# GpSimd instead of VectorE for the copies of weight slots in a linear-attention and mixture-of-experts kernel

## The chip, the cores and the metric

One core of a Trainium2 chip. The metric is the time of one execution on the device in microseconds (us); lower is better. Each result lists the granted TensorE clock (1.0 is full).

## The reference, cut to what matters

```python
kv  = einsum('bhsd,bhse->bhde', k, v)            # 8 sentences, 8 heads, 576 rows, 64 wide
out = einsum('bhsd,bhde->bhse', q, kv)
x   = out / sqrt(mean(out*out) + 1e-6) * g_norm  # -> 8 x 576 x 512
e   = argmax(mean_over_rows(x) @ w_gate)         # one expert per sentence, of 8
h   = maximum(x @ w1[e], 0)                      # w1[e]: 512 x 1024
y   = gate_weight * (h @ w2[e])                  # w2[e]: 1024 x 512
```

With the inputs used, the experts of sentences 0 to 7 are 4 4 7 6 5 1 3 1. Sentence 1 repeats sentence 0's expert and sentence 7 repeats sentence 5's.

## The kernel before

The weights of a sentence live in one of three slots of W1 and W2. Expert numbers are only known on the chip. So before each load of weights, the kernel copies the slot of one of the two preceding sentences into the sentence's own slot, and then loads from HBM over it, unless the expert is the same as one of the two:

```python
def s_w(b, i):                                   # b: sentence, i: W1 or W2
    own = b % NW
    W = (W1, W2)[i]
    cond = None
    if b > 0:
        if b > 1 and i == 0:
            st[b]["sv"] = nc.values_load(st[b]["src"][0:1, 0:1],
                                         engines=(mybir.EngineType.DVE,), ...)
        sv = st[b].get("sv", 0)                  # sentence 1: always slot 0
        for h in range(2):
            n = W.shape[2] // 2
            nc.vector.tensor_copy(W[:, own, h * n:(h + 1) * n],
                W[:, ds(sv, 1), h * n:(h + 1) * n].rearrange("p o c f -> p (o c) f"))
        for e in evs[max(0, b - 2):b]: ...       # cond: expert differs from both
    ...
        nc.gpsimd.dma_start(W[:, own, :, fs], (moe_w1, moe_w2)[i][ds(ev, 1), :, fs]..., cond=cond)
```

The kernel gives each engine its instructions in the order of a fixed list (`ORDER`). Steps, with the names that the profile gives their outputs: `qr` (VectorE re-packs q, SBUF to SBUF), `o` (attention output out of PSUM), `xT` (VectorE: `o` times `rs`, two SBUF inputs), `tw` and `ts` (VectorE: the gate's product and sum; `tw` has two SBUF inputs), `lg` (GpSimd's power operation, from which VectorE makes the gate), `m_1` and `m_2` (TensorE: the two matrix products with W1 and W2, profile lines L352 and L392).

```python
nc.vector.scalar_tensor_tensor(out=part(s["xT"][:, c, :], h), in0=s["o", c, h], scalar=gcol,
                               in1=part(s["rs", c], h), op0=ALU.mult, op1=ALU.mult, ...)   # xT
nc.vector.tensor_tensor(tw, wg, s["pl"][:, 0:NP].unsqueeze(2).to_broadcast(...), ALU.mult)  # tw
nc.gpsimd.tensor_tensor(lg, base, st[b]["dl"], ALU.pow)                                    # lg
```

Of the kernel before, what the change touches and what calls it, by code (L numbers as in the profile page):

```python
# [50 lines left out]
def kernel(  # L51
# [11 lines left out]
    nc = tc.nc  # L63
# [28 lines left out]
    st = [dict() for _ in range(B)]  # L92
# [209 lines left out]
    def s_w(b, i):  # L302
# [3 lines that stand above are left out]
        if b > 0:  # L306
            if b > 1 and i == 0:
                st[b]["sv"] = nc.values_load(
                    st[b]["src"][0:1, 0:1], engines=(mybir.EngineType.DVE,), min_val=0,
                    max_val=NW - 1,  # L310
                    skip_runtime_bounds_check_because="it is one of two numbers of slots")
            sv = st[b].get("sv", 0)
            for h in range(2):
                n = W.shape[2] // 2
                nc.vector.tensor_copy(  # L315
                    W[:, own, h * n:(h + 1) * n],
                    W[:, ds(sv, 1), h * n:(h + 1) * n].rearrange("p o c f -> p (o c) f"))
            for e in evs[max(0, b - 2):b]:
                c = evs[b] != e
                cond = c if cond is None else s_logical_and(cond, c)  # L320
        ev = evs[b]
        nh = {0: 4, B - 1: 2}.get(b, 1) if i == 0 else 1
        n = W.shape[3] // nh
        for h in range(nh):
            fs = slice(h * n, (h + 1) * n)
            nc.gpsimd.dma_start(W[:, own, :, fs], (moe_w1, moe_w2)[i][ds(ev, 1), :, fs]  # L326
                                .rearrange("o (c p) f -> p (o c) f", p=P), cond=cond)
# [93 lines left out]
    def emit(tok):  # L421
# [10 lines left out]
        elif f == "R":  # L432
            cast_first(c)
        elif f == "P":
            st[0]["row"] = sm.tile([1, E], F32, tag="row", name="row")
            nc.vector.tensor_copy(st[0]["row"], st[0]["pg"])
            ps0.__exit__(None, None, None)
            psp[0] = ctx.enter_context(tc.tile_pool(name="ps", bufs=2,
                                                    space=bass.MemoryType.PSUM))
            first[0] = False  # L440
        elif f == "K":
            s_kv(b, [c] if b == 0 else range(NP))
        elif f == "C":
            s_tc(b, c)
        elif f == "G":
            if (b, c) == (0, 1):
                s_row()
            else:
                (s_gate, s_gate2, s_gate3, s_gate4)[c](b)
        elif f == "Q":  # L450
            s_qr(b)
        elif f == "W":
            s_w(b, c)
        elif f == "L":
            load_qkv(b, 1, only=(c,))
        elif f == "T":
            s_qt(b, c, x)
        elif f == "O":
            s_o(b, c, h, x)
        else:  # L460
            dict(M=s_m, X=s_x)[f](b, c, h)
# [33 lines left out]
```

## Time and profile before

| | before |
|---|---|
| time, three runs | 194.69, 194.96, 196.69 us |
| span of the profiled run, clock | 191.0 us, 0.995 |
| busy: TensorE, VectorE, ScalarE, GpSimd | 170.8, 110.8, 106.6, 50.4 us |

The prediction below shows the lines and reads them.

### The profile page before, as it was taken

To read this page: it belongs to the slowest core of one execution; us is meant where nothing else is said; L and a number is where in the kernel's file an instruction comes from. 1 tells how busy PE (TensorE), PEld (TensorE's weight loads), DVE (VectorE), ACT (ScalarE), POOL (GpSimd) and SP (SyncE) were. 2 spreads that over 40 slices of the span, in tenths; PEclk is the share of its full clock that TensorE was granted. 3 is DMA by queue.
4 is the path that set the end of the run, shared out by engine and by line. 5 is a ranking of instruction groups with operands and counts; after the bars stand their busy time and mean duration, and the time that the engine had idled before them with its cause. 6 is when DMAs were issued, how large, how long until landed. Compare 5 with 4: busy or idle time off the path is not lost.

```text
span 191.0 us, 4338 instructions
## 1 busy us (share of the span) xinstructions
PE 170.8 (89%) x1691; PEld 113.0 (59%) x1691; DVE 110.8 (58%) x289; ACT 106.6 (56%) x168; POOL 50.4 (26%) x64
## 2 busy tenths in 40 slices
PE   0297787998999999899999999999999999999991
PEld 0253255775578755686568746867586568457541
DVE  2437374878878795585565785697754482332010
ACT  2146107767877767676666655675257656316512
POOL 7670098018305130016127020311022103000000
PEclk9999999999999999999999999999999999999998
DMA  5999999999999999999999999999999799062045
GB/s 157 194 202 205 201 200 189 206 208 201 229 239 246 205 207 240 255 228 203 221 259 235 205 217 243 264 188 170 239 260 187 154 158 210 18 160 76 0 113 134
DMA packets 37030, 36.91 MB, mean 193 GB/s; under 512 B 2706, under 2 KB 30354, under 8 KB 37010
## 3 DMA queue, kind: packets, MB, share of 16 engines
q0 software_dynamic: 29328, 26.30, 86.4%
q1 hardware_dynamic: 7394, 9.98, 18.2%
q10 hardware_dynamic: 288, 0.36, 0.7%
q8 instruction: 13, 0.21, 0.4%
q14 instruction: 7, 0.06, 0.1%
HBM read 61.88 MB, written 9.44 MB: 373 GB/s over the span
## 4 chain that ended last, share of the span: by engine, by line
PE 58%; DMA 23%; DVE 6%; issue 5%; ACT 4%; POOL 2%; POOLq 0%; DVEq 0%
PE ps_m L352 27%; PE ps_m L392 21%; DMA W<-in_moe_w_dram 12%; DMA qt<-in_q_dram 7%; DMA kt<-in_k_dram 4%; DVE o L179 3%; ACT sq L212 3%; PE ps_a L224 3%; PE ps_a L207 2%; PE ps_m L379 2%; PE ps_a L160 2%; DVE W L315 1%; PE ps_a L192 1%; POOL qt L103 1%; DVE qr L174 1%
## 5 line engine op out<-in xcount | busy, mean ns | idle before, releaser
L352 PE MATMUL ps_m<-xT,W 128*128 128x288 f16 x512 | 68.2, 286 | 1.2 <-DMA W<-in_moe_w_dram 1.2
L392 PE MATMUL ps_m<-W,hT 128*128 128x512 f16 x256 | 60.7, 379 | 0.0
L352 PEld LDWEIGHTS <-W 128*128 128x128 f16 x512 | 49.4, 98 | 13.9 <-DMA W<-in_moe_w_dram 1.6
L359 ACT ACTIVATE hT<-ps_m 128x576 f16<-128x576 f32 x51 | 33.2, 652 | 21.5 <-PE ps_m L352 21.3
L392 PEld LDWEIGHTS <-hT 128*128 128x128 f16 x256 | 24.2, 98 | 24.5 <-ACT hT L359 0.6
L326 POOL DMA_DIRECT2D W<-in_moe_w_dram x20 | 12.5, 628 | 74.6 <-DMA W<-in_moe_w_dram 16.5
L363 ACT ACTIVATE ot<-ps_m,gates 128x512 f32<-128x512 f32 (+1 forms) x26 | 17.0, 656 | 18.2 <-PE ps_m L392 12.9
L228 ACT ACTIVATE rs<-ps_a,epsc 128x576 f32<-128x576 f32 x28 | 20.5, 741 | 7.2 <-PE ps_a L224 6.7
L237 DVE SCALAR_TENSOR_TENSOR xT<-o,gcol,rs 128x576 f16<-128x576 f32 x28 | 22.4, 811 | 3.5 <-ACT rs L228 3.4
L212 ACT ACTIVATE sq<-ps_a 128x576 f16<-128x576 f32 x28 | 17.9, 648 | 10.6 <-PE ps_a L207 10.5
L179 DVE COPY o<-ps_a 128x576 f32<-128x576 f32 x20 | 15.0, 757 | 15.2 <-ACT sq L212 14.9
L277 POOL TENSOR_TENSOR lg<-base,dl 128x8 f32<-128x8 f32 x8 | 14.7, 1836 | 27.2 <-DVE src L296 17.7
L365 DVE TENSOR_SCALAR ot<-ps_m,gates 128x512 f32<-128x512 f32 (+1 forms) x14 | 9.4, 673 | 18.5 <-PE ps_m L392 16.6
L315 DVE COPY W<-W 128x2048 f16 (+1 forms) x28 | 19.3, 695 | 1.4 <-DVE src L296 0.5
L179 ACT COPY qT<-ps_a 128x576 f16<-128x576 f16 x15 | 9.5, 636 | 10.7 <-PE ps_a L160 10.7
L356 DVE TENSOR_SCALAR hT<-ps_m 128x576 f16<-128x576 f32 x13 | 9.8, 755 | 8.7 <-PE ps_m L352 8.7
L192 PEld LDWEIGHTS <-kt 96*64 96x64 f16 x384 | 7.5, 116 | 9.9 <-ACT kt L179 5.8
L224 PE MATMUL ps_a<-sq,ones 128*128 128x288 f16 x56 | 11.1, 286 | 2.1 <-DVE o L179 2.0
L207 PE MATMUL ps_a<-qT,kvb 128*128 128x288 f16 x56 | 11.3, 286 | 1.2 <-DVE o L179 0.8
L103 POOL DMA_DIRECT2D kt<-in_k_dram x10 | 7.5, 750 | 12.7 <-PE ps_m L352 12.4
L224 PEld LDWEIGHTS <-ones 128*128 128x128 f16 x64 | 6.0, 99 | 7.9 <-issue 3.2
L160 PEld LDWEIGHTS <-qr 96*128 96x128 f16 x144 | 8.7, 98 | 2.7 <-issue 0.4
(75 smaller groups left out, 138.1 us busy)
## 6 DMA issues: line engine op xcount, KB each, us to landing
W<-in_moe_w_dram POOLq DMA_DIRECT2D x14, 1024.0 KB, 14.1
out_dram<-ot SPq DMA_DIRECT2D x24, 192.0 KB, 5.7
qt<-in_q_dram POOLq DMA_DIRECT2D x7, 576.0 KB, 14.6
kt<-in_k_dram POOLq DMA_DIRECT2D x7, 576.0 KB, 10.4
vt<-in_v_dram POOLq DMA_DIRECT2D x7, 576.0 KB, 16.1
out_dram<-ot SPq DMA_DIRECT2D x39, 64.0 KB, 5.6
out_dram<-ot SPq DMA_DIRECT2D x16, 128.0 KB, 5.2
W<-in_moe_w_dram POOLq DMA_DIRECT2D x4, 256.0 KB
```

Of the source, the lines that this page charges most:

```text
L179: nc.scalar.copy(out, in_) if x else nc.vector.tensor_copy(out, in_)
L207: nc.tensor.matmul(po[:, i, 0:HS], kvb[:, b % 2, c, :], s["qT"][:, c, i * HS:(i + 1) * HS], start=True, stop=True)
L212: nc.scalar.activation(part(s["sq", c], h), po, AF.Square)
L224: nc.tensor.matmul(pm[:, i if h is None else 0, 0:HS], ones, s["sq", c][:, i * HS:(i + 1) * HS], start=True, stop=True)
L228: nc.scalar.activation(part(s["rs", c], h), pm[:, 0:2 if h is None else 1, 0:HS], AF.Abs_reciprocal_sqrt, bias=epsc)
L237: nc.vector.scalar_tensor_tensor(out=part(s["xT"][:, c, :], h), in0=s["o", c, h], scalar=gcol, in1=part(s["rs", c], h), op0=ALU.mult, op1= ...
L277: nc.gpsimd.tensor_tensor(lg, base, st[b]["dl"], ALU.pow)
L315: nc.vector.tensor_copy(W[:, own, h * n:(h + 1) * n], W[:, ds(sv, 1), h * n:(h + 1) * n].rearrange("p o c f -> p (o c) f"))
L352: nc.tensor.matmul(ph[:, i, 0:HS], w1[:, c, fb * P:(fb + 1) * P], s["xT"][:, c, i * HS:(i + 1) * HS], start=(c == 0), stop=(c == 3))
L359: nc.scalar.activation(two(s["hT"][:, fb, :]), ph[:, :, 0:HS], AF.Relu)
L363: nc.scalar.activation(out, in_, AF.Copy, scale=gates[:, b:b + 1])
L392: nc.tensor.matmul(po[:, 0, :], s["hT"][:, fc, t * P:(t + 1) * P], w2[:, fc, :], start=(fc == 0), stop=(fc == 7))
```

## The change

Its intent: take 19 us of copies off VectorE and give them to an engine that is idle three quarters of the time, and that issues the loads behind the copies anyway. The whole diff:

```diff
                 st[b]["sv"] = nc.values_load(
-                    st[b]["src"][0:1, 0:1], engines=(mybir.EngineType.DVE,), min_val=0,
+                    st[b]["src"][0:1, 0:1], engines=(mybir.EngineType.Pool,), min_val=0,
 ...
             for h in range(2):
                 n = W.shape[2] // 2
-                nc.vector.tensor_copy(
+                nc.gpsimd.tensor_copy(
                     W[:, own, h * n:(h + 1) * n],
                     W[:, ds(sv, 1), h * n:(h + 1) * n].rearrange("p o c f -> p (o c) f"))
```

## The prediction

In it and in the expectations further down, "the port" and "the lock" stand for one thing: an instruction of VectorE and one of GpSimd that overlap hold each other up. The trace of the kernel before showed this in the power operation alone (1.67 and 2.48 us), and the ten waits of 1 us are my estimate.

> **What bounds the kernel now.** I read the busy row of each engine first. VectorE, which the change relieves, is busy 58% of the 191.0 us span, GpSimd 26%, TensorE 89%. So the first question is whether VectorE's copies matter to anyone. The slices show which two things are full.
>
> ```profile
> PE   0297787998999999899999999999999999999991
> DVE  2437374878878795585565785697754482332010
> POOL 7670098018305130016127020311022103000000
> DMA  5999999999999999999999999999999799062045
> ```
>
> One slice is 4.8 us. From about 33 us TensorE is at nine or more nearly always, and the DMA engines are at nine up to about 145 us. VectorE is never full for long. The kernel is bound by TensorE, with the loads close behind it; from 140 us on there is only TensorE. The view of waits says how often TensorE stood still for a load of weights:
>
> ```profile
> PE ps_m L352 <- DMA W<-in_moe_w_dram: 1.2, 2, 0.9
> PE ps_a L224 <- DVE o L179: 2.0, 3, 1.1
> ```
>
> Two waits for weights, 1.2 us in all. By windows they are one of 0.9 us at 78 us (sentence 2's first weights) and one of 0.3 us at 137 us (sentence 5's). The waits on VectorE's o copy lie mostly (1.5 of 2.0 us) before 50 us, near or before the first weight copy at 48.8 us, so most of them cannot be the copies' fault.
>
> Next, the copies, the loads and the power operation on GpSimd, in the list of groups:
>
> ```profile
> L315 DVE COPY W<-W 128x2048 f16 (+1 forms) x28 | 19.3, 695 | 1.4 <-DVE src L296 0.5
> L326 POOL DMA_DIRECT2D W<-in_moe_w_dram x20 | 12.5, 628 | 74.6 <-DMA W<-in_moe_w_dram 16.5
> L277 POOL TENSOR_TENSOR lg<-base,dl 128x8 f32<-128x8 f32 x8 | 14.7, 1836 | 27.2 <-DVE src L296 17.7
> ```
>
> There are 28 copies (seven sentences, two matrices, two halves), 0.695 us each, 19.3 us of VectorE. GpSimd sits idle 74.6 us before its weight loads. Setting VectorE's and GpSimd's timelines side by side, every load of weights from sentence 2 on is issued 0.3 to 0.6 us after the second half of its copy ends. So the copy gates each load, and the copy itself starts when VectorE's program order comes to it. The chain of waits shows the one place where that matters for the end:
>
> ```profile
> 124.19 0.32 DVE o L179
> ...
> 124.86 0.70 DVE W L315
> 125.56 0.02 issue
> 125.58 0.70 DVE W L315
> ...
> 126.92 10.18 DMA W<-in_moe_w_dram
> 137.11 0.05 issue
> 137.16 2.87 PE ps_m L352 x22
> ```
>
> The columns are start, length, what. Two copies, 0.6 us to the issue, a 10.18 us load, and TensorE begins sentence 5 the moment it lands. After it TensorE is busy without a gap of note to the end, so what is lost here is lost from the time.
>
> [...] No GpSimd copy is in this trace, but there are three small stand-ins.
>
> ```profile
> 3.52 0.23 POOL masks.py:197 MEMSET ident<- 128x128 f16 x1
> 3.81 0.29 POOL masks.py:199 TENSOR_SCALAR_AFFINE_SELECT ident<-ident 128x128 f16<-128x128 f16 x1
> 0.46 0.11 POOL L479 MEMSET const-uint8-127<- 128x1 uint8 x1
> ```
>
> From one element (0.093 to 0.113 us, mean 0.104) to 128 elements (0.225 and 0.295 us in the list of groups) the slope is 0.95 ns and 1.50 ns an element[...]. [...] the power operation takes 1.67 us when undisturbed, and 2.48 us where VectorE's four qr copies (59.03 to 60.18 us) lie on it.
>
> ```profile
> 59.23 2.48 POOL L277 TENSOR_TENSOR lg<-base,dl 128x8 f32<-128x8 f32 x1 [1.42 <-DVE src L296]
> 122.54 1.67 POOL L277 TENSOR_TENSOR lg<-base,dl 128x8 f32<-128x8 f32 x1 [7.49 <-DVE src L296]
> ```
>
> **The change part by part.** Removed from VectorE: 28 x 0.695 = 19.3 us, leaving 110.8 - 19.3 = 91.5 us, 48% of the old span. Added to GpSimd: 28 copies of 2048 elements. At 0.95 ns: 0.104 + 2048 x 0.00095 = 2.05 us; at 1.50 ns: 3.18 us. I choose 2.05, since the copy has nothing to compute, and keep 3.18 as the bad case. 28 x 2.05 = 57 us, so GpSimd goes from 50.4 to about 108 us, 55% of the span. It is not full, but it also issues all loads of q, k, v and weights in order, so a copy pair of 4.1 us stands ahead of whatever comes next on it.
>
> Moved: the copy no longer waits for VectorE's program order, but for GpSimd's, and starts as soon as GpSimd gets to it. For each load I took GpSimd's last act before it in the old timeline, added about 0.4 us to read the slot number (0.29 us is what such a register load takes in the trace), 4.1 us for the pair and 0.6 us to the issue:
>
> - Sentence 2, first weights: power ends near 61, issue near 66.2; it was 65.45. Late by 0.8. The loads ahead of it (issued 51.77, landing after up to 20.4 us) keep the queue fed to about 71, so nothing is lost.
> - Sentence 3: the k load's issue ends 83.8, so 88.9; it was 86.78. Late by 2.1. The queue is fed to 91.3 (82.97 + 8.3). With some 2.7 us between an issue and its first data (my estimate, below), slack is 1.8, so 0.3 us is lost.
> - Sentence 4: late by some 3.5, with two older loads queued ahead and TensorE not there before 117 us. Nothing.
> - Sentence 5: source number at 122.38, power to 124.21, then 124.6 + 4.1 + 0.6 = 129.3; it was 126.92. Late by 2.4, of which up to 0.4 may hide, so 2.0.
> - Sentences 6 and 7: late by 1 to 3, but TensorE comes to them more than 3 us after they land, and is itself pushed back by the 2 us. Nothing.
>
> That sentence 5 has no slack is shown by the DMA in windows of 1 us (last two columns: DMA share, GB/s). The last v load is issued at 114.28 and lands after 15.4 us, at 129.7, and the rate sags there already:
>
> ```profile
> 127.00:128.00 1.00, 1.00 (x6) 0.49 (x5) 0.86 (x4) 0.97 (x2) 0.73 (x1) 1.00 1.25 194
> 128.00:129.00 1.00, 1.00 (x7) 0.43 (x5) 0.97 (x3) 0.27 (x1) 0.00 (x0) 1.00 1.22 135
> 129.00:130.00 1.00, 1.00 (x8) 0.65 (x7) 0.52 (x1) 0.58 (x2) 0.00 (x0) 1.00 0.86 147
> 130.00:131.00 1.00, 1.00 (x11) 0.54 (x8) 0.39 (x1) 1.00 (x2) 0.87 (x1) 1.00 1.16 201
> ```
>
> So the queue ran nearly dry about 2 us after the issue at 126.92 and filled again near 130: that is where the 2.7 us comes from.
>
> Then the port. About ten of the 28 xT operations of VectorE (two SBUF inputs each, 0.811 us) should meet a GpSimd copy and wait 1 us on average: 10 us back of the 19 us saved. They stand ahead of the o copies that free TensorE's banks, so I put 0.5 us on the path. Sum: 2.0 + 0.3 + 0.5 = 2.8 us, 194.96 + 2.8 = 197.8 us.
>
> **The rivals.** First, a gain: the copies leave VectorE's queue, o copies and gates come sooner. For it: the chain has a copy pair of 1.20 us at 56.5 us in front of an o copy. Against: the saved time there runs into the wait at 78 us, which is set by the backlog of loads, and TensorE waited on o only 0.5 us after 50 us. If a GpSimd copy took only 1 us[...], sentence 5 would issue at 127.2, and the time stays at 195 or falls by half a us. Second, a copy of 3.18 us: sentence 5 then issues at 131.5, late by 4.6; sentence 3 at 91.2, 2.6 lost; with more port waits, 7 to 8 us, about 202 us; GpSimd busy about 140 us and nearly the second bound. Third, the load is hidden anyway: if the queue still has work at 130 us, nothing changes at all, and the time stays within 0.5 us of 195.
>
> **Range and chances.** I give 2.05 us a copy (1.8 to 2.3) about half, 3 us a quarter, 1.2 us or less an eighth. That makes a middle of 197.8, and 195.2 to 202.0 as the range. Slower by over 2% begins at 198.9, which needs copies of about 2.5 us or more, or port waits of 2 us on the path: 0.34. Faster by over 2% would need a bound that VectorE sets, and none is seen: 0.03.
>
> **What will show it.** The copy's duration in the groups on GpSimd: 2.05 right, 1 or 3 wrong. The issue of sentence 5's first weights near 129.3 instead of 126.9, and TensorE's wait on weights there about 2.3 instead of 0.3 us. The mean of xT above 0.811 us, or VectorE's idle time in front of it grown. If TensorE's new idle time names o or xT rather than weights, the port is the larger cost; if the new wait is at sentence 2 or 3, my backlog estimate is wrong; if TensorE waits for nothing new, the third rival holds.

## The result and the profile after

The changed kernel took 204.46 us in the median of four runs (202.63 to 206.85), against 194.82 us (four runs). The ratio is 1.048, 95% interval 1.036 to 1.061: slower. A ratio here is the mean time of one kernel's fast runs over that of the other's fast runs of the same rounds, so it is not quite the ratio of the medians.

The slices of the span, changed kernel (one slice is 5.1 us):

```profile
PE   0298796998795999999969999999989999899992
DVE  1346354777997546675591789473953254021010
POOL 7750276009973599009965974089539901870000
PEclk9999767999997999999999999999999999999999
```

GpSimd is now often full. New and not foreseen is the last row: the clock granted to TensorE sags in slices 4 to 6 (about 20 to 35 us), before any copy of weights runs, and once more in slice 12. Then the groups of instructions:

```profile
L315 POOL COPY W<-W 128x2048 f16 (+1 forms) x28 | 56.3, 2016 | 7.4 <-PE ps_m L352 5.4
L237 DVE SCALAR_TENSOR_TENSOR xT<-o,gcol,rs 128x576 f16<-128x576 f32 x28 | 33.5, 1216 | 5.4 <-ACT rs L228 5.4
```

In the kernel before, the line of xT reads:

```profile
L237 DVE SCALAR_TENSOR_TENSOR xT<-o,gcol,rs 128x576 f16<-128x576 f32 x28 | 22.4, 811 | 3.5 <-ACT rs L228 3.4
```

A copy takes 2.02 us on average (its median by line is 1.90), as predicted. But xT, whose code did not change, went from 811 to 1216 ns. The chain of waits, changed kernel, shows where that matters:

```profile
50.00 3.58 DVE qr L174 x4
53.58 3.84 DVE xT L237 x6
...
59.62 3.09 DVE tw L244
62.74 0.21 DVE ts L246
62.98 0.47 DVE qT L179
63.49 0.58 PE ps_a L207 x2
```

From 50 to 63 us the path to the end runs through VectorE. In the kernel before it runs through TensorE there up to 55 us, and through VectorE only from 55.8 to 58.9. The operation tw on 32 elements a partition takes 3.09 us; its median is 0.19. The timeline of the changed kernel shows what lay beside it:

```profile
58.92 3.73 POOL L315 COPY W<-W 128x2048 f16<-128x2048 f16 x2
59.62 3.08 DVE L244 TENSOR_TENSOR tw<-wg,pl 128x32 f32<-128x32 f32 x1
```

tw begins during sentence 1's second pair of GpSimd copies and ends, at 62.70, with it. TensorE's waits in the changed kernel (us in total, times, longest) name VectorE more than the weights:

```profile
PE ps_a L207 <- DVE qT L179: 3.4, 2, 2.3
PE ps_m L352 <- DMA W<-in_moe_w_dram: 0.5, 2, 0.3
```

**Stages.** To see where time went I cut each trace at the first m_1 matmul of each sentence in TensorE's timeline. Uneventful stages repeat to a few hundredths of a us, whatever the total does and on whichever of three chips the rounds ran, so this is a far finer instrument than the total. "Again" means a second trace of the same kernel; the last column of each row ends the span.

| us | start to 0 | 0 to 2 | 2 to 3 | 3 to 4 | 4 to 5 | 5 to 6 | 6 to 7 | 7 to end | span |
|---|---|---|---|---|---|---|---|---|---|
| before | 30.85 | 47.62 | 19.31 | 19.48 | 19.90 | 17.83 | 16.08 | 19.98 | 191.0 |
| before, again | 36.44 | 47.84 | 19.30 | 19.48 | 19.98 | 17.82 | 16.05 | 19.97 | 196.9 |
| changed | 33.59 | 53.27 | 21.35 | 19.48 | 21.32 | 17.98 | 16.68 | 19.95 | 203.6 |
| changed, again | 31.02 | 50.36 | 21.03 | 19.67 | 21.34 | 17.82 | 17.53 | 19.98 | 198.7 |

Three readings. The start varies by 5.6 us between two traces of the *unchanged* kernel, with half clock and later first loads in the slow one; that is chance. Of the changed kernel's loss, 2.5 to 2.7 us lie between sentences 0 and 2 where the clock stays full (5.4 to 5.7 where it sags), 1.7 to 2.0 between 2 and 3, 1.4 between 4 and 5, and 0.6 to 1.5 between 6 and 7. At full clock that is 7.7 us of span (198.7 against 191.0).

The stretch from 0 to 2 hides part of the loss. From sentence 0 to 1 alone, at full clock throughout, the kernel before takes 25.14 us and the changed kernel (again) 28.90: 3.8 us more. In the next stage 1.0 us comes back (22.48 against 21.46), because there the kernel before waits 0.9 us for sentence 2's weights.

### The profile page after: what moved, and what is told of

The parts are those of the page before. It is cut to its first block, busy times and chain, and to the rows that moved or that the text cites. A ratio compares the mean times of both kernels' runs of the same rounds, so it can differ in the third digit from the quotient of the medians.

```text
span 203.6 us, 4362 instructions
## 1 busy us (share of the span) xinstructions
PE 178.0 (87%) x1691; PEld 115.6 (57%) x1691; DVE 108.5 (53%) x261; ACT 107.0 (53%) x168; POOL 106.3 (52%) x92
## 4 chain that ended last, share of the span: by engine, by line
PE 59%; DMA 14%; DVE 12%; issue 5%; POOL 5%; ACT 3%; POOLq 1%; ACTq 0%
PE ps_m L352 24%; PE ps_m L392 17%; DMA W<-in_moe_w_dram 10%; POOL W L315 4%; DMA vt<-in_v_dram 3%; DVE o L179 3%; PE ps_a L207 2%; PE ps_a L224 2%; DVE xT L237 2%; ACT sq L212 2%; PE ps_a L149 2%; PE ps_m L379 2%; PE ps_kv L149 2%; PE ps_a L192 2%; DVE qr L174 2%
## 5 line engine op out<-in xcount | busy, mean ns | idle before, releaser
L352 PE MATMUL ps_m<-xT,W 128*128 128x288 f16 x512 | 70.7, 292 | 0.5 <-DMA W<-in_moe_w_dram 0.5
L315 POOL COPY W<-W 128x2048 f16 (+1 forms) x28 | 56.3, 2016 | 7.4 <-PE ps_m L352 5.4
L352 PEld LDWEIGHTS <-W 128*128 128x128 f16 x512 | 50.5, 100 | 14.6 <-issue 0.8
L237 DVE SCALAR_TENSOR_TENSOR xT<-o,gcol,rs 128x576 f16<-128x576 f32 x28 | 33.5, 1216 | 5.4 <-ACT rs L228 5.4
L207 PEld LDWEIGHTS <-kvb 128*128 128x128 f16 x64 | 5.9, 103 | 9.8 <-issue 6.5
L160 PE MATMUL ps_a<-ident,qr 96*128 96x96 f16 x144 | 10.4, 209 | 1.1 <-ACT o L179 1.1
```

What stands on the lines that cost most here:

```text
L207: nc.tensor.matmul(po[:, i, 0:HS], kvb[:, b % 2, c, :], s["qT"][:, c, i * HS:(i + 1) * HS], start=True, stop=True)
L315: nc.gpsimd.tensor_copy(W[:, own, h * n:(h + 1) * n], W[:, ds(sv, 1), h * n:(h + 1) * n].rearrange("p o c f -> p (o c) f"))
L352: nc.tensor.matmul(ph[:, i, 0:HS], w1[:, c, fb * P:(fb + 1) * P], s["xT"][:, c, i * HS:(i + 1) * HS], start=(c == 0), stop=(c == 3))
```

## The experiments

I had two theories. **Late loads**: the long copy on GpSimd delays the loads queued behind it. **The port**: while a GpSimd copy runs, VectorE's operations with two SBUF inputs and its qr copies stand still, and what follows them comes late. In the changed kernel an xT took up to 3.00 us (median 0.82), tw up to 3.08 (median 0.19), and a qr copy up to 2.70 (median 0.35; at most 0.60 before). The traces show such durations and not how they come about, so "port" and "lock" are names and no more. Each edit below is to the changed kernel unless it says otherwise. All results were correct. Clocks are given in brackets.

**after_again.** No edit.

> The changed kernel once more, to see what of its 9.6 us is the same each time. Its first trace had TensorE at half clock from 23.5 to 29 us, before any weight copy runs, some 2.8 us. If that dip is chance: absent here or at another place, and the time 201 to 203. If the change brings it about in some way that I don't see: there again, and about 204. In both, the stretch from the first m_1 matmul of sentence 0 to that of sentence 2 is about 5 to 6 us longer than in the kernel before.

Measured: 200.43 (1.0), 200.72 (0.991), 204.97 (0.966) and 205.94 us (0.965). The early dip is absent in the profiled run and the time 200.4: chance, in both kernels, since seven runs of the kernel before in the same rounds read 193.93 to 195.28 at clocks of 0.999 and 1.0, and 196.31 to 199.39 at 0.957 to 0.974. The stage from 0 to 2 is 50.36, so 2.5 to 2.7 us over before, half of what I expected. The other 2.9 us of the first trace's loss there are half clock, in two parts: 1.4 us by the end of the early dip, which lasts to 36.28 us and so reaches into the stage from 0 to 1, and 1.5 us by the second dip. Windows of that trace at the second dip; after the window's length comes TensorE's busy time, and the third number from the end is the granted clock:

```profile
62.00:64.00 2.00, 0.51 (x3) 0.38 (x3) 1.93 (x4) 0.00 (x0) 0.69 (x2) 0.90 1.18 283
64.00:66.00 2.00, 2.00 (x10) 1.18 (x9) 0.86 (x2) 0.65 (x1) 0.00 (x0) 0.50 1.28 226
66.00:68.00 2.00, 2.00 (x15) 1.46 (x14) 0.28 (x3) 1.09 (x2) 0.00 (x0) 0.75 1.23 254
```

TensorE stood for 2.30 us up to 63.49, and then ran at half clock until 67: in this trace the granted clock is 0.50 from 22.62 to 29.44 us, from 32.86 to 36.28 and from 63.58 to 67.00. In the second trace TensorE stood as long, 2.32 us (57.35 to 59.67), and the clock stayed at 1.00. The same stop brought half clock in one run and not in the other; what decides it these traces do not show.

**s1_vector, s1_gpsimd.** Sentence 1's four copies back on VectorE and the other 24 on GpSimd, and the reverse:

```diff
-                nc.gpsimd.tensor_copy(
+                (nc.gpsimd if b != 1 else nc.vector).tensor_copy(     # s1_vector
+                (nc.gpsimd if b == 1 else nc.vector).tensor_copy(     # s1_gpsimd
```

> Only sentence 1's four copies go back to VectorE, the other 24 stay on GpSimd. Theory of the port: sentence 1's copies hold up VectorE's qr copies, xT and tw between 50 and 63 us, and TensorE with them (5.7 us of shift there), so this run gains about 5 us over the changed kernel: 198 to 200. Rival, late loads: sentence 1 loads nothing, only the later loads count, and this run stays within 1.5 us of the changed kernel.

> The complement: only sentence 1's four copies on GpSimd, the others on VectorE. Theory of the port: 5 to 6 us slower than the kernel before, about 200. Rival, late loads: within 1 us of the kernel before, about 195.

Measured: s1_vector 196.41 to 198.03 us (0.982 to 0.991), ratio 1.0095 (0.9999 to 1.019); s1_gpsimd 197.67 (1.0) and 200.13 to 201.18 (0.974 to 0.987), ratio 1.022 (1.010 to 1.035). In stages: with sentence 1 on VectorE the stretch 0 to 2 is 47.95, as before. With it alone on GpSimd it is 51.99 (28.87 of it from 0 to 1, at full clock), with a 2.3 us stop of TensorE and half clock after it once more (0.50 from 64 to 66 us); this trace is of a slow run. Sentence 1 loads nothing, so its own loads cannot be the cause in this stage. That it is the port is tested below, in dummy_copy and dummy_memset. s1_vector gains less than 5 us on the changed kernel at equal clock, about 4 (196.5 against 200.6): I had taken the clock dip for part of the port.

**split8.** Eight pieces instead of two:

```diff
-            for h in range(2):
-                n = W.shape[2] // 2
-                nc.gpsimd.tensor_copy(W[:, own, h * n:(h + 1) * n], ...)
+            for h in range(8):          # cs, fs: eight pieces of 512 elements
+                nc.gpsimd.tensor_copy(W[:, own, cs, fs], W[:, ds(sv, 1), cs, fs]...)
```

> All copies on GpSimd as in the change, but each matrix in 8 pieces of 512 elements, not 2 of 2048. Theory of the port[...]: VectorE waits at most about 0.55 us instead of 1.9, the xT mean falls from 1.22 to 0.95 us or less, and the time falls by 3 us or more, to about 200, though the copies take some 0.8 us more in all per matrix. Rival, late loads: the time rises by 0.5 to 2 us.

Measured: 207.04 to 211.04 us (0.934 to 0.966), ratio 1.061 (1.050 to 1.072). My expectation missed. The port's part came true: the mean of xT fell from 1.22 to 0.90 us and the stretch 0 to 2 to 48.39, in which 0 to 1 took 25.13 us, as in the kernel before. But GpSimd paid for it: one matrix took 5.3 to 6.6 us instead of 3.8 to 4.3 in sentences 2 to 5. Waits and the pieces in the run's trace:

```profile
PE ps_m L354 <- DMA W<-in_moe_w_dram: 7.3, 3, 3.9
133.38 5.73 POOL L317 COPY W<-W 128x512 f16 x8
```

TensorE now waited 7.3 us for weights. Cutting the copies traded VectorE's standstill for late loads, at a loss.

**dummy_copy, dummy_memset.** The kernel before, its copies on VectorE, plus work for nobody on GpSimd beside sentence 1's copies:

```diff
+            if b == 1:
+                for h in range(2):
+                    nc.gpsimd.tensor_copy(scr, W[:, 0, half h])      # dummy_copy
+                    nc.gpsimd.memset(scr, float(h))                  # dummy_memset
             for h in range(2):
                 n = W.shape[2] // 2
                 nc.vector.tensor_copy(
```

> The kernel before, with all its copies on VectorE, and beside sentence 1's copies four GpSimd copies of the same size into an unused tile. Nothing waits for their result; sentence 1 loads no weights, so no load of weights is made late by them directly. Theory of the port: VectorE is held up as in the change, qr, xT and tw stretch, and the time is 3 to 6 us over the kernel before. Rival, the copy's place in GpSimd's order: TensorE does not wait for the unused tile, and the time stays within 1 us.

> As dummy_copy, but the four instructions are memsets of the same 2048 elements, which read nothing (about 2 us each by the slope of the small memsets). If the lock is on reading, xT and tw, which have two SBUF inputs, keep their 0.81 and 0.19 us, and at most the qr copies stretch: within 1.5 us of the kernel before. If any long GpSimd instruction holds VectorE up: as dummy_copy. If GpSimd's being busy is what counts (the two loads behind it late): as dummy_copy too, with VectorE's durations unchanged.

Measured: dummy_copy 196.69 (0.994) to 201.0 us (0.970); dummy_memset 193.26 (1.0) and 194.18 (0.989) to 197.39 (0.974), ratio 0.993 (0.983 to 1.003). The two instructions keep GpSimd busy almost equally long (2.09 and 1.86 us each). What they do to tw, first in dummy_copy, then in dummy_memset (minimum, median, maximum in ns):

```profile
L245 DVE TENSOR_TENSOR tw<-wg,pl x7: 181/191/1873, 40.7 to 161.5; 128x32 f32<-128x32 f32 x7
```

```profile
L245 DVE TENSOR_TENSOR tw<-wg,pl x7: 181/191/193, 42.6 to 161.6; 128x32 f32<-128x32 f32 x7
```

A copy nobody waits for holds tw up for 1.7 us, and one xT for 1.6; a memset of the same size leaves both alone (xT mean 0.810), although tw (at 58.20) and two xT (at 52.21 and 52.94) ran during memsets (50.16 to 54.03 and 58.01 to 61.69). The qr copies stretched equally in both (mean 0.45 instead of 0.38 us). So in these two traces the standstill of the two-input operations comes from the GpSimd instruction's *reading*, and neither from GpSimd being busy nor from the two loads behind it. The stretch 0 to 2 is 49.92 in dummy_copy, about 2 us over before, less than the 3 to 6 that I expected. In dummy_memset's trace it is 49.16, 1.3 over, while the run at full clock, 193.26 us, leaves no room for that. Its trace fell in a slow run (197.33, 0.974), so what the held qr copies cost by themselves, between nothing and 1.3 us, stays open.

**s1_first, s1_second.** As s1_gpsimd, but only sentence 1's first (W1) or second (W2) pair on GpSimd; one look each.

```diff
+                (nc.gpsimd if (b, i) == (1, 0) else nc.vector).tensor_copy(   # s1_first; (1, 1): s1_second
```

> Only sentence 1's first pair on GpSimd. qr and one xT stretch (by 2.1 and 1.6 us). Stages from sentence 0's to sentence 2's first m_1 matmul: 47.6 to 47.9 us before, about 50.4 with both pairs at full clock. If tw is what counts: 48.5 or less here. If the qr and xT delays count: 49 to 50.

> Only sentence 1's second pair on GpSimd. tw stretches from 0.19 to 2 us or more if it still meets a copy. If tw is what counts: the two stages sum to 49.5 us or more, nearly as with both pairs. If the first pair's delay is needed for that meeting (GpSimd and VectorE then stand elsewhere): below 48.5.

Measured: 197.71 us (0.974) and 197.09 us (0.997). The stretch 0 to 2 was 49.26 and 49.95, against 47.6 to 47.8 before and 50.4 with both. Either pair costs, and the costs (about 1.5 and 2.2) do not add up. The first stretched qr and one xT as expected (3.66 and 2.43 us), and TensorE then waited 1.1 us for an o copy. In the second the copies came earlier than in the changed kernel, missed tw (0.19 us) and hit an xT instead:

```profile
53.53 4.71 DVE L237 SCALAR_TENSOR_TENSOR xT<-o,gcol,rs 128x576 f16<-128x576 f32 x1 [0.33 <-ACT rs L228]
53.89 3.73 POOL L315 COPY W<-W 128x2048 f16<-128x2048 f16 x2
```

This xT, 0.81 us elsewhere, stood through *both* copies, though its record starts 0.36 us before theirs, and TensorE stood behind it for 3.2 us. So it is not tw as such that costs: a two-input operation of VectorE is caught somewhere (tw for 3.08 us in the changed kernel, this xT for 4.71), and the one caught is the one that TensorE's next matmul needs.

**w1_late.** The changed kernel with one step moved, `1W1x` from before to after `2G2x` in the list of steps.

```diff
-    "... 3T3 3O0 1W1x "   "0m12x 3O2 1m0 1m7 2G1x 1m2 2G2x 3M0x ..."
+    "... 3T3 3O0 "        "0m12x 3O2 1m0 1m7 2G1x 1m2 2G2x 1W1x 3M0x ..."
```

> The changed kernel with one step moved: sentence 1's second pair of GpSimd copies after sentence 2's power operation, so that it cannot lie on sentence 2's tw any more. Theory of the port at this place: tw there is back at 0.19 us, the stage from sentence 0's to sentence 1's first m_1 matmul is 2 to 3 us shorter than in the changed kernel, and the time 1 to 3 us better, about 198, as sentence 2's loads are issued about 1 to 3 us later behind the copies. Rival, the sum of GpSimd's work counts: no better than the changed kernel, about 200.5.

Measured: 200.69 (0.991), 204.16 (0.992), 204.56 (0.983) and 207.96 us (0.958); the fastest is no better than the changed kernel's. The trace is that of the 204.16 run, slow, so I use it only for what the moved step touches. tw was back at 0.19 and the stage from 0 to 1 fell from 28.90 to 26.41 us, as expected. But the next stage rose from 21.46 to 25.03, since sentence 2's loads were issued late and the queue ran dry; windows, last column GB/s:

```profile
68.00:72.00 4.00, 4.00 (x74) 2.76 (x73) 2.03 (x5) 2.24 (x4) 3.34 (x4) 1.00 1.20 185
72.00:76.00 4.00, 4.00 (x32) 2.25 (x31) 2.72 (x6) 2.83 (x5) 3.68 (x3) 1.00 0.26 47
```

**s1_s3_vector.** Sentences 1 and 3 on VectorE (`b not in (1, 3)`). The reason is this timeline of VectorE in s1_vector, between sentences 2 and 3:

```profile
92.32 0.16 DVE L340 TENSOR_REDUCE gs<-lg 128x1 f32<-128x8 f32 x1 [2.50 <-POOL lg L277]
92.51 0.17 DVE L341 RECIPROCAL gates<-gs 128x1 f32<-128x1 f32 x1
92.59 3.01 DVE L237 SCALAR_TENSOR_TENSOR xT<-o,gcol,rs 128x576 f16<-128x576 f32 x1
...
95.90 2.06 DVE L237 SCALAR_TENSOR_TENSOR xT<-o,gcol,rs 128x576 f16<-128x576 f32 x1
```

The power operation lg stands behind sentence 3's first pair of copies on GpSimd; VectorE waits 2.5 us for it, and is then caught twice by the second pair.

> The copies of sentences 1 and 3 on VectorE, the other 20 on GpSimd. In the run with sentence 1 alone on VectorE, the power operation of sentence 3 came late behind a copy, VectorE waited 2.5 us for it, and two xT operations behind it took 3.0 and 2.1 us. If that is what the stage at 90 to 100 us loses, this run is 1 to 1.5 us faster than that run at the same clock, about 195.5, and the loss left is sentence 5's and later. If the late loads of sentence 3 were the cause instead: also faster, but with VectorE's xT times there unchanged.

Measured: 196.36 (0.987) to 198.02 us (0.969), ratio 1.016 (1.009 to 1.022). The total does not show a gain over s1_vector (medians 196.98 and 197.09; no run had a clock of 0.99), but the stage does: 19.72 us instead of 20.87, against 19.3 before. The 0.4 us left end, by its chain of waits, in a load of sentence 3's first weights.

**s5_gpsimd, s5_first, s5_second.** Only sentence 5 on GpSimd: all four copies, its first pair, its second pair.

```diff
+                (nc.gpsimd if b == 5 else nc.vector).tensor_copy(             # s5_gpsimd
+                (nc.gpsimd if (b, i) == (5, 0) else nc.vector).tensor_copy(   # s5_first; (5, 1): s5_second
```

> Only sentence 5's four copies on GpSimd, the others on VectorE. This is the term that the prediction put at 2.0 us: its first load should be issued near 129 us instead of 127 and TensorE should wait about 2 us for it. Late loads: 1.5 to 2.2 us slower than the kernel before at the same clock. Port alone: VectorE's xT near 125 us waits, but no load of weights is later, and the time is within 0.5 us.

> Only sentence 5's first pair of copies on GpSimd. Late load: issue near 129.2, and the stage from sentence 4's to sentence 5's first m_1 matmul is 21.0 to 21.3 us, as with all four copies, against 19.9 to 20.0 in the kernel before. Port alone: 19.9 to 20.3.

> Only sentence 5's second pair on GpSimd. Late load: that stage stays at 19.9 to 20.1 us, though two xT operations stretch to about 1.2 and 2.4 us. Port: 21.0 to 21.3.

Measured: s5_gpsimd 194.47 (1.0), 194.97 (1.0), 195.20 (0.991) to 197.94 us, ratio 1.003 (0.995 to 1.011); s5_first 200.58 us (0.963), s5_second 193.69 us (0.989). Stage 4 to 5: 21.20, 22.10 and 19.82 us, against 19.90. So a late load is enough to cost this stage time (s5_first). It is not shown to be the only cause, and the lock is not shown to be free here. In s5_gpsimd TensorE stood 1.1 us in the stage: 0.7 us for ts and 0.3 for ot, both VectorE's. The late weights landed at 138.77, and m_1 began at 138.90; VectorE's delay and the load's ended nearly together. s5_second does not test the lock: of the two xT that were to stretch only one did, to 1.21 us. GpSimd in s5_gpsimd, and TensorE's wait in the stage in s5_first:

```profile
124.62 4.25 POOL L315 COPY W<-W 128x2048 f16 x2
129.19 0.81 POOL L326 DMA_DIRECT2D W<-in_moe_w_dram  x1 [0.32 <-POOL W L315]
```

```profile
PE ps_m L352 <- DMA W<-in_moe_w_dram: 2.2, 1, 2.2
```

The copy starts at 124.62 and the load is issued at 129.19; the prediction said 124.6 and 129.3. That match is partly luck: lg starts 0.44 us later here than in the prediction's trace (122.98, not 122.54), and the copy began as lg ended, without the 0.4 us that the prediction added for reading the slot number. Counted from sentence 4's first m_1, the load was issued after 11.49 us, against 9.66 in the kernel before, so it was late by 1.8 us and not by 2.4. After its wait of 2.2 us TensorE fell to half clock again in s5_first (0.50 from 144 to 146 us), and the stage from 5 to 6 took 19.48 instead of 17.83.

**load_always, copies_1_7.** Looking for a version that beats both: the kernel before, with copies on VectorE only for sentence 1, or only for 1 and 7, and a plain load in place of the others. Both are right for any data.

```diff
-        if b > 0:
+        if b == 1:              # load_always
+        if b in (1, B - 1):     # copies_1_7
```

> The kernel before without any copy from sentence 2 on; their weights are always loaded, so the result is right for any data, at the cost of one more load of both matrices for sentence 7 here. All copies gone from VectorE: if they cost anything there or in front of the loads, this is faster: sentence 5's first load is issued near 125 us instead of 127, the wait at 137 us goes away, 0.3 to 1.5 us faster than the kernel before. If sentence 7's new loads come late, slower by as much as TensorE then waits near 171 us.

> For a version that beats both: the kernel before with copies (on VectorE) only for sentences 1 and 7, and a plain load for the rest; right for any data, and with this data no load more than before. Against the run that always loads, sentence 7's late weights (a wait of 1.6 us) are gone: 1 to 2 us faster than the kernel before at the same clock, about 193.

Measured: load_always 192.95 (0.991) to 197.61 us, ratio 0.994 (0.982 to 1.006); copies_1_7 192.70 (0.991) and 192.95 (0.996) to 196.93 us, ratio 0.994 (0.986 to 1.002). Neither is shown to be faster. From sentence 0's to sentence 7's first m_1 matmul they take 139.98 and 140.42 us; the two traces of the kernel before 140.22 and 140.47. Twenty-four and twenty copies fewer on VectorE, and the same time: VectorE's copies were free, within some 0.5 us (the stage from 4 to 5 took 19.37 us in load_always and 19.87 in copies_1_7, against 19.90). I expected 0.3 to 2 us and there is none that I can show. The risk named for load_always came true: sentence 7's new load arrived late, TensorE waited 1.6 us for it, and the rest after sentence 7's first m_1 took 21.76 us instead of 19.98.

**before_again.** The kernel before, unedited.

> The kernel before once more, for a second trace of it: its timed runs show granted clocks from 0.95 to 1.0. If the half-clock dip at 23 to 30 us is chance of any kernel, a run of this one at a clock near 0.97 is 2 to 3 us slower than one at 1.0 (about 194). In its trace the weight copies, xT and tw keep 0.69, 0.81 and 0.19 us.

Measured: 198.74 (0.963) and 198.73 us (0.955). Both runs were granted a low clock, and the comparison gives this kernel a ratio to *itself* of 1.024 (1.016 to 1.033). Its trace has half clock from 22 to 32 us, and 0.50 again from 36 to 38. So a difference of under 2% in the ratios above says nothing by itself, without the clocks; I rest no argument on one.

## Why the prediction was wrong

The direction was seen, the size was not: 197.8 predicted, with 202.0 as the upper end, and 204.46 measured. At full clock, where the changed kernel's two runs read 200.43 and 200.72 us and the kernel before's mostly 192.7 to 195.3, the loss is about 6.5 us, against 2.8 predicted.

- **The copy** (2.05 us chosen): right, 1.90 undisturbed, 2.7 times VectorE's 0.69, and 2.02 in the mean. The memsets that served as stand-ins were fair ones (1.86 us for a memset of the copy's size). GpSimd's busy time of 106.3 us met the predicted 108.
- **Sentence 5's load** (late by 2.4, 2.0 on the path): right in place, too large, and not alone. The load was late by 1.8 us, and the stage lost 1.4 us in the changed kernel, 1.3 in s5_gpsimd and 2.2 in s5_first. The sign that the prediction named, a wait of about 2.3 us for weights, came in s5_first only. In the changed kernel TensorE waited 0.7 us for VectorE's ts there and then 0.2 us for the weights.
- **"Then the port. ... so I put 0.5 us on the path"**: this is the step that failed. The amount of standstill was not far off: VectorE was busy 108.5 us, so 17.0 us over the 91.5 of its own work, where I allowed 10. Missing from my count were tw and the qr copies. The share of it on the path was wrong, nearly 4 us instead of 0.5: 2.5 to 2.7 us up to sentence 2, and 1.2 of the 1.7 to 2.0 between sentences 2 and 3 (20.87 in s1_vector against 19.72 in s1_s3_vector; lg's late start is part of these 1.2). I spread ten waits evenly and argued with averages. What counts is the one operation caught ahead of TensorE's next matmul, and I had not followed sentence 1's copies to their neighbours at all, because sentence 1 loads nothing. My list of terms began with sentence 2.
- **Sentence 3** (0.3 us by a late load): the late load was about that (0.4 in s1_s3_vector). Not seen was that the power operation itself stands behind the copy pair, and VectorE, in its fixed order, behind the power operation (for 2.5 us in s1_vector).
- **Sentences 6 and 7** ("Nothing"): 0.6 and 1.5 us in the two traces of the changed kernel, 0.0 in s1_vector. In the second trace TensorE waits 1.4 us for sentence 6's second weights; why this load was late there and not in s1_vector was not settled.
- **The clock**: not in the prediction. The early dip is chance that both kernels share. The later one is a cost that the change brings in some runs: half clock followed in two of the three traces in which sentence 1's copies stopped TensorE for 2.3 us, and took about 1.5 us in each (23.00 and 23.13 us from sentence 1 to 2, against 21.46). In the third, after_again, it did not follow, nor after s1_second's stop of 3.2 us (clocks of 1.0 and 0.997 over these traces). What decides it was not shown.
- **The rivals**: "the load is hidden anyway" fell. "A gain" fell for the reason given, and load_always shows it directly. The prediction's own test, "if TensorE's new idle time names o or xT rather than weights, the port is the larger cost", gave the right answer.

## What to carry to other kernels

Work moved from a busy engine to an idle one is worth something only if the busy engine sets the end; ask first what taking the work away altogether would gain, here nothing. Before giving GpSimd a long instruction that reads SBUF, list what stands beside it and behind it: VectorE's two-input operations (an xT of 0.81 us took up to 4.71 here) and its copies within SBUF (a qr copy of 0.35 took up to 2.70), the loads in GpSimd's own queue (sentence 5's came 1.8 us late), and the small operation that another engine is waiting for (lg, for 2.5 us). And cut traces into stages before comparing totals, for chance can be as large as the effect: the unchanged kernel read 192.7 to 200.7 us, at clocks of 0.954 to 1.0 (the 200.7 at 0.991, so the clock is not all of it).
